# Two row streams on one core: the side work handed out by a count of VectorE's and ScalarE's time per chunk

## The chip, the core and the metric

One core of a Trainium2 chip runs the whole kernel. The metric is the device time of one execution in microseconds; lower is better. TensorE (PE) does the matrix products, VectorE (DVE) and ScalarE (ACT) the elementwise work, GpSimd (POOL) nearly nothing, and the sync engine (SP) issues the transfers.

## What is computed

The reference, cut to what matters:

```python
# attention: a causal convolution of 7 softmaxed taps per head, 8 heads of 24 columns
w = softmax(weight)                               # (8, 7)
x = einsum('hk,bskhg->bshg', w, windows_of(x))    # (2, 4096, 192)
x = x.reshape(8192, 192)
# layer 1
h = x @ moe_w_in                                  # (8192, 2048)
x = (h * clip(h + 3, 0, 6) / 6) @ moe_w_out       # (8192, 192)
# layer 2
h = x @ moe2_w_in
out = where(h > 0, h, exp(min(h, 0)) - 1) @ moe2_w_out
```

The inputs `x`, `w_in`, `w_out` of the two layers arrive as 64-bit floats, in two 32-bit words each.

## The kernel before

**Tiling.** The 8192 tokens are 16 blocks of 512 (half from each batch). The 2048 hidden columns are 16 groups of 128. A **chunk** is one group of one block of one layer: there are 2 x 16 x 16 = 512, listed in `slots` and numbered from 0. Layer 1's first blocks come first; from chunk 112 on, 16 chunks of layer 2 and 16 of layer 1 alternate; from chunk 400 on there is layer 2 alone. Every fp32 product is made of rounded (fp32r) high and low parts, so a chunk has 5 matrix products of 128 rows in `mm1` (input to hidden, with the operands opA to opD of the block) and 5 in `mm2` (hidden to output).

**Two streams.** Up to chunk 35 the matmuls use all 128 rows of the array (`whole_rows`). From chunk `BOTH + LAG` = 36 on, each product is cut into its lower and upper 64 rows, and two streams of matmuls (`lower_rows`, `upper_rows`) are issued in turn, so that a pair runs side by side. The lower stream makes the lower half of `h` in a PSUM bank, a one-element memset on POOL (`relay`, one per chunk) hands the bank on, and the upper stream adds its half. `h` has three banks (`ps_h`, `bufs=3`): the lower stream can begin chunk s + 3 only when chunk s's bank has been read.

**The main work of a chunk** on the other engines (`gate`, `split_g`): ACT makes `u` from `h`, DVE makes `g` from `u` and `h` (this frees the bank), ACT rounds the `g` of the chunk before to `gh`, and DVE makes `gl`, the remainder. In layer 2 ACT has a second pass over `u`, the exponential. `mm2` of a chunk follows five chunks later.

**The side work** also runs on DVE and ACT. It is (a) the convolution of later blocks (`conv`): per block two transposes on DVE, two products on ACT, six tap steps of 512 and six of 256 on DVE (`acc`), then ACT's copies to opA, opD, opC, DVE's remainders opB, opC, opD, and ACT's last two copies; (b) decoding and splitting the weights (`decode`, `split_w`), part by part: ACT `xw` and DVE `cw` from the raw words, DVE joins them in `xw`, ACT rounds (`wi1h`, `wi1r`, `wo`), DVE makes the remainder; (c) the sums of the two accumulators and the output transposes (`first_sum`, `second_sum`, `store`); (d) layer 2's operands (`split_y`). Both engines work in the order in which their instructions are issued.

**The planner.** Each piece of side work is a generator; a step is what it issues up to the next `yield`. After each chunk's main work `run_jobs(s)` issues steps: first those whose due chunk has come (`last(jb)`), then, as every job earns credit at its rate (cost left over chunks left), the job with the most credit, until the credits together are at most `STEP` = 300. A step's cost is DVE's metered work plus a fifth of ACT's (`step`, class `Meter`: fixed 80 or 90 plus the elements of a row). `LATER` after a step keeps the job from being stepped again in the same chunk, but from chunk 128 on only (`at[0, RA, 0]`), and not when it is due. The weights' rate comes from `due(item)`, the chunk that first needs the part. Order on the engines is as issued from chunk 36 on (`manual_schedule`); before that a scheduler places the instructions.

Of the kernel before, what the change touches and what calls it, by code (L numbers as in the profile page):

```python
# [18 lines left out]
LAG = 4  # L19
LAG2 = LAG + 1  # L20
# [7 lines left out]
ACT_LOW = range(5, 9)  # L28
R_CUTS = ((4, 4, 8), (8,))
STEP = 300  # L30
NB = 512
HB = NB // 2
SQ = 32
# [23 lines left out]
def conv_moe_moe2(ctx: ExitStack, tc: tile.TileContext, x, weight, w_in1, w_out1, w_in2, w_out2, out):  # L57
# [26 lines left out]
    assert 2 * R == P and B == 2  # L84
    JT = NB // P
    LO, UP, ALL = slice(0, R), slice(R, P), slice(0, P)
    NBLK = NT // NB

    vec, act = Meter(nc.vector, 80), Meter(nc.scalar, 90)
# [28 lines left out]
    def word(raw, i):  # L118
        return raw.rearrange("p (n two) -> p n two", two=2)[:, :, i]

    def decode(raw, n, meanwhile, low_by_vec):
# [3 lines left out]

        xw = tmp.tile([P, NB], F32, name="xw", tag="xw")
        act.activation(xw[:, :n], word(raw, 1).bitcast(F32), AF.Prelu, scale=2.0 ** -112, alpha=2.0 ** 32)
        c = tmp.tile([P, NB], I32, name="cw", tag="cw")
        low = word(raw, 0).bitcast(U32)
# [12 lines left out]
    def load_w(item):  # L142
        kind, l, a, e = item
        t = stage.tile([P, 2 * NB], I32, name="raw", tag="raw")
        if kind == "out":
# [15 lines left out]
    def split_w(item, f):  # L161

        kind, l, a, e = item
        if kind == "out":
            v = f[:, :(e - a) * D].rearrange("p (f e) -> p f e", f=e - a)
            w = wo[l][:, a:e]
            act.copy(w[:, :, 0:D], v)
            yield  # L170
            for c0, c1, to in ((0, P, 2 * P), (P, D, D)):
                vec.tensor_tensor(out=w[:, :, to:to + c1 - c0], in0=v[:, :, c0:c1],
                                  in1=w[:, :, c0:c1].bitcast(F32), op=ALU.subtract)
            yield
            return
        w = {k: v[:, a * P:e * P] for k, v in wi[l].items()}
        if kind == "in":
            f = f[:, :(e - a) * P]
            act.copy(w["h"], f)
            yield  # L180
            vec.tensor_tensor(out=w["l"], in0=f, in1=w["h"].bitcast(F32), op=ALU.subtract)
        else:
            f = f[:, :(e - a) // 2 * P].rearrange("p (f c) -> p f c", c=P)
            r = w["r"].rearrange("p (f two c) -> p two f c", two=2, c=P)
            for k, h in enumerate((LO, UP)):
                act.copy(r[h, k], f[h])
            yield
            for k, h, o in ((0, LO, UP), (1, UP, LO)):
                vec.tensor_tensor(out=r[o, k], in0=f[h], in1=r[h, k].bitcast(F32), op=ALU.subtract)
        yield  # L190


# [366 lines left out]
    def mm2(s, half, which=(0, 1, 3, 2, 4), cols=slice(0, NB)):  # L559

        l, b, f = slots[s]
        gh, gl = gs[s]
        w = wo[l][half, f, :]
        first, last = f == 0, f == NF - 1
        if first:
            acc[l, b, half is UP] = [ps_o.tile([P, NB], F32, name=f"p{i}", tag="po") for i in range(2)]
        p0, p1 = acc[l, b, half is UP]
        w0h, wr, w0l = (w[:, k * P:(k + 1) * P] for k in range(3))
        todo = [(p0, w0h, gh, 0), (p0, w0l, gh, 0), (p1, wr, gh, 0), (p0, w0h, gl, 1), (p1, wr, gl, 1)]
        for i in which:  # L570
            p, k, m, end = todo[i]
            n = R + 2 if k is wr and end and not last else P
            nc.tensor.matmul(p[:n, cols], k[:, :n], m[half, cols], start=first and not end and k is not w0l,  # L573
                             stop=end == 1 and (last and cols.stop == NB or s == NS - 2 and half is UP and p is p0))
            yield
# [11 lines left out]
    at = {sl: i for i, sl in enumerate(slots)}  # L587
# [17 lines left out]
    def step(jb, s):  # L605
        w = vec.work, act.work
        said = next(jb[2], jobs)
        done = said is jobs
        if said is LATER and s >= at[0, RA, 0]:
            jb[8] = s  # L610
        cost = vec.work - w[0] + (act.work - w[1]) // 5
        jb[4] += 1
        jb[6] += cost
        jb[7] -= cost
        if done:
            jobs.remove(jb)

    def load(item):

        kind, _, a, e = item  # L620
        n = (e - a) * {"out": D, "in": P, "r": R}[kind]
        lo = {"out": n + 160, "in": n + 80, "r": 2 * n + 160}[kind]
        return n // 2 + 80 + n + 80 + lo + (2 * n + 180) // 5

    def run_jobs(s):

        def last(jb):
            return jb[0]() - (1 if jb[0]() <= BOTH else 2)

        def rate(jb):  # L630
            if jb[3]:
                return max(jb[5] - jb[6], 0) / max(last(jb) - s, 1)
            need, most = 0, 0
            for k in range(ready[0], len(items)):
                need += load(items[k]) * (1 - min(steps[0], 3) / 4 if k == ready[0] else 1)
                most = max(most, need / max(due(items[k]) - LEAD - 1 - s, 1))
            return most

        for jb in sorted(jobs, key=lambda j: j[0]()):
            while jb in jobs and (s >= last(jb) or not jb[5] and jb[3] and s >= jb[1]):  # L640
                step(jb, s)
        for jb in jobs:
            if s >= jb[1]:
                jb[7] += rate(jb)
        while True:
            going = [j for j in jobs if s >= j[1] and s > j[8]]
            if sum(j[7] for j in going) <= STEP:
                break
            step(max(going, key=lambda j: j[7]), s)

    def whole(*gens):
        for g in gens:
            yield from g

    def drain(gen):
        for _ in gen:
            pass

    def due(item):
        kind, l, a, e = item  # L660
        return at[l, 0, a] + ((LAG, LAG2 - 2)[l] if kind == "out" else 0)

    def when(i):

        if i >= len(items):
            return 0
        return due(items[i]) - LEAD
# [42 lines left out]
    def prepare():  # L710

        last = iter(())
        for i, item in enumerate(items):
            ahead(i)
            n = (item[3] - item[2]) * {"out": D, "in": P, "r": R}[item[0]]
            f = yield from counted(decode(raws.pop(i), n, last, i not in ACT_LOW))
            ready[0], steps[0] = i, 0
            last = split_w(item, f)
            next(last)
        yield from last  # L720
        ready[0] = len(items)
# [45 lines left out]
    for b in range(2, NBLK):  # L767
        e = at[0, b, 0] - 2
        if b <= RA:
            t = at[0, b - 1, 0]  # L770
            if b > 2:
                t, e = t - 2, e + (b < RA)
            else:
                t += NF // 2
        else:
            t = at[0, b - 1, 0] - 8
            e = at[0, b - 1, NF - 1]
        job(feed(b), 1, t - 8, t - 7)
        job(whole(squares(b), conv(b)), 2 + CONV, t, e, WORK["conv"])
    for b in range(NBLK):  # L780
        e = at[1, b, 0]
# [57 lines left out]
    BOTH = at[0, 2, 0]  # L839

    def whole_rows():

        for s in range(BOTH + LAG):
            yield from mm1(s, ALL)
            first_done(s)
            if s >= LAG:
                yield from seconds_with(s - LAG, ALL)
# [28 lines left out]
    def lower_rows():  # L876

        two = seconds(LO)
        for s in range(BOTH + LAG, NS):
            yield from mm1(s, LO)  # L880
            if s >= BOTH + LAG2:
                yield from some(two, 5)
        yield from two

    def upper_rows():

        two = seconds(UP)
        yield from some(two, HEAD)
        for s in range(BOTH + LAG, NS):
            yield from mm1(s, UP)  # L890
            first_done(s)
            if s >= BOTH + LAG2:
                yield from some(two, 5)
        yield from two

    drain(whole_rows())
    with tc.manual_schedule():
        ends = {}
        n = {LO: 0, UP: HEAD}
        for half in (LO, UP):  # L900
            for s in range(BOTH + LAG, NS):
                assert half is LO or n[half] > ends[s]
                n[half] += 5 if (half is LO) == (slots[s][2] % 2 == 0) else 4
                if half is LO:
                    ends[s] = n[half]
                n[half] += 5 * (s >= BOTH + LAG2)
        going = [lower_rows(), upper_rows()]
        while going:
            for g in list(going):
                if next(g, jobs) is jobs:  # L910
                    going.remove(g)
        for k in range(B):
            drain(mm2(NS - 1, ALL, (0, 1, 3), slice(k * HB, (k + 1) * HB)))
        last_store(NBLK - 1, *(acc.pop((1, NBLK - 1, up)) for up in (False, True)))
        run_jobs(NS + 9)
# [30 lines left out]
```

## Time and profile before

| what | value |
|---|---|
| median of 3 runs | 1141.55 us (1141.54 to 1142.05) |
| the profiled execution, its own time | 1141.55 us |
| its span, first to last instruction | 1139.7 us |
| outside the span | 1.85 us |
| PE busy | 1127.6 us, 99% |
| VectorE, ScalarE busy | 81%, 82% |
| granted TensorE clock | 0.999 of full speed |

A row of the timeline gives start, duration, engine, line, operation, tiles (out<-in), shape, count and, in brackets, the engine's idle time before and what ended it. An instruction's duration includes its write-back, which overlaps the next one: queued instructions of 512 columns that last 0.69 us start 0.60 us apart. For sums along a queue the distance from start to start is used.

### The profile page before, as it was taken

How to read it: one execution, taken by the hardware profiler on the slowest of the kernel's cores; microseconds unless marked ns; L12 is line 12 of the kernel's file. 1: busy time of each engine (PE TensorE's matmuls, PEld its weight loads, DVE VectorE, ACT ScalarE, POOL GpSimd, SP SyncE). 2: the span in 40 equal slices, each digit the busy share in tenths (PEclk: the TensorE clock that was granted, in tenths of full speed). 3: DMA queues.
4: the chain of work that ended last, by engine and by line, in shares of the span. 5: the costliest groups of instructions: out<-in, count | busy, mean ns of one | idle time of the engine just before them, and what ended most of it. 6: DMA issues, size and time to landing. Idle time of an engine off the chain costs nothing.

```text
span 1139.7 us, 25118 instructions
## 1 busy us (share of the span) xinstructions
PE 1127.6 (99%) x9490; PEld 1065.4 (93%) x9490; DVE 918.5 (81%) x1558; ACT 935.1 (82%) x1699; POOL 44.5 (4%) x491
## 2 busy tenths in 40 slices
PE   8999999999999999999999999999999999999998
PEld 6787989888899999999999999999999999999997
DVE  7998999998887868779687887878867677777675
ACT  8877877778878787887878878787886899899886
POOL 0000000000000000000000000000000000000000
PEclk9999999999999999999999999999999999999999
DMA  6411121010010100101001010000000000000001
GB/s 188 108 53 42 36 49 44 29 29 1 2 29 1 21 10 2 29 1 29 2 7 23 1 29 1 16 15 1 16 1 15 2 1 16 15 15 15 9 7 28
DMA packets 105369, 26.79 MB, mean 24 GB/s; under 512 B 96416, under 2 KB 104096, under 8 KB 105248
## 3 DMA queue, kind: packets, MB, share of 16 engines
q1 hardware_dynamic: 104960, 24.99, 10.3%
q8 instruction: 74, 1.21, 0.4%
q14 instruction: 47, 0.39, 0.1%
q10 hardware_dynamic: 288, 0.20, 0.1%
HBM read 18.87 MB, written 6.29 MB: 22 GB/s over the span
## 4 chain that ended last, share of the span: by engine, by line
PE 92%; ACT 4%; DVE 3%; issue 1%; DMA 0%; ACTq 0%; SPq 0%; DVEq 0%
PE p L573 48%; PE h L527 44%; ACT u L51 1%; DVE g L51 1%; DVE gl L51 1%; DVE acc L51 0%; ACT gh L51 0%; ACT opC L51 0%; ACT xw L51 0%; ACT opD L51 0%; ACT diagl L51 0%; ACT xT L51 0%; DMA x_sq<-in_x_dram 0%; ACT acc L51 0%; DVE s L51 0%
## 5 line engine op out<-in xcount | busy, mean ns | idle before, releaser
L573 PE MATMUL p<-gh,wo 64*128 64x512 f32 (+1 forms) x2976 | 717.2, 386 | 0.0
L573 PE MATMUL p<-gl,wo 64*128 64x512 f32 (+2 forms) x1984 | 601.5, 386 | 0.0
L51 DVE SCALAR_TENSOR_TENSOR g<-u,h 128x512 f32<-128x512 f32 x512 | 350.4, 685 | 184.6 <-ACT u L51 178.2
L573 PEld LDWEIGHTS p<-gh,wo 64*128 64x128 f32 (+1 forms) x2976 | 412.9, 184 | 27.9 <-ACT gh L51 1.1
L51 DVE TENSOR_TENSOR gl<-g,gh 128x512 fp32r<-128x512 f32 x512 | 350.5, 685 | 1.9 <-ACT gh L51 1.6
L51 ACT CAST gh<-g 128x512 fp32r<-128x512 f32 x512 | 311.9, 609 | 9.6 <-DVE g L51 9.2
L51 ACT ACTIVATE u<-h,three 128x512 f32<-128x512 f32 x256 | 176.1, 688 | 107.7 <-PE h L527 105.3
L573 PEld LDWEIGHTS p<-gl,wo 64*128 64x128 f32 (+2 forms) x1984 | 252.6, 160 | 6.7 <-DVE gl L51 0.2
L51 ACT ACTIVATE u<-h 128x512 f32<-128x512 f32 x256 | 152.7, 597 | 57.5 <-PE h L527 56.2
L527 PE MATMUL h<-opA,wi1l 64*128 64x512 f32 x512 | 198.0, 387 | 0.0
L527 PE MATMUL h<-opA,wi1h 64*128 64x512 f32 x512 | 197.9, 386 | 0.0
L527 PE MATMUL h<-opB,wi1h 64*128 64x512 f32 x512 | 197.6, 386 | 0.0
L527 PE MATMUL h<-opA,wi0h 64*128 64x512 f32 (+1 forms) x476 | 183.9, 390 | 2.4 <-DVE g L51 2.1
L527 PE MATMUL h<-opA,wi0l 64*128 64x512 f32 (+1 forms) x476 | 183.3, 388 | 0.0
L527 PE MATMUL h<-opB,wi0h 64*128 64x512 f32 (+1 forms) x476 | 182.7, 387 | 0.0
L51 ACT ACTIVATE u<-u 128x512 f32<-128x512 f32 x256 | 161.9, 633 | 7.6
L527 PE MATMUL h<-opC,wi1r 64*128 64x512 f32 x384 | 148.2, 386 | 0.0
L527 PE MATMUL h<-opD,wi1r 64*128 64x512 f32 x384 | 148.2, 386 | 0.0
L527 PE MATMUL h<-opC,wi0r 64*128 64x512 f32 (+1 forms) x366 | 141.0, 387 | 0.7 <-ACT opC L51 0.6
L527 PE MATMUL h<-opD,wi0r 64*128 64x512 f32 (+1 forms) x366 | 140.8, 387 | 0.0
L51 DVE SCALAR_TENSOR_TENSOR acc<-xT,taps,acc 128x256 f32<-128x256 f32 (+1 forms) x180 | 106.8, 603 | 0.1
L527 PEld LDWEIGHTS h<-opA,wi0h 64*128 64x128 f32 (+1 forms) x476 | 87.6, 184 | 11.3 <-DVE g L51 6.5
(108 smaller groups left out, 1220.5 us busy)
## 6 DMA issues: line engine op xcount, KB each, us to landing
raw<-in_moe_w_out_dram SPq DMA_DIRECT2D x16, 384.0 KB, 3.2
out_dram<-z SPq DMA_DIRECT2D x180, 32.0 KB, 1.7
x_sq<-in_x_dram SPq DMA_DIRECT2D x112, 32.0 KB, 2.1
raw<-in_moe_w_in_dram SPq DMA_DIRECT2D x7, 512.0 KB, 3.9
raw<-in_moe_w_in_dram SPq DMA_DIRECT2D x8, 256.0 KB, 4.0
xr_sq<-in_x_dram SPq DMA_DIRECT2D x56, 32.0 KB, 2.1
x_sb<-in_x_dram SPq DMA_DIRECT2D x4, 128.0 KB, 2.9
raw<-in_moe_w_in_dram SPq DMA_DIRECT2D x4, 128.0 KB, 3.2
```

The lines of the kernel that those rows point to most:

```text
L51: return fn(*args, **kw)
L527: mm = nc.tensor.matmul(h, k, m[half], start=low and i == 0, stop=high and i == len(todo) - 1)
L573: nc.tensor.matmul(p[:n, cols], k[:, :n], m[half, cols], start=first and not end and k is not w0l, stop=end == 1 and (last and cols.stop = ...
```

## The change

1. A count `booked` of the metered work of VectorE and of ScalarE runs along; each chunk takes `SLOT` = 2153 from it. In `run_jobs` the handing-out by credit also stops when either engine's count has reached `SLOT` (`full`), from chunk 36 on. Steps that are due are issued as before.
2. `due` of layer 2's weights is twelve chunks sooner (`SOON` = 12), which raises the weights' rate in all rounds.
3. Layer 2's remainders of `wi1r` are two steps, one for each half (`yield` in `split_w`).
4. One more round of `run_jobs`, for chunk 35, at the start of the row-split stage.

```diff
--- before.py
+++ after.py
@@ -28,6 +28,8 @@
 ACT_LOW = range(5, 9)
 R_CUTS = ((4, 4, 8), (8,))
 STEP = 300
+SLOT = 2153
+SOON = 12
 NB = 512
 HB = NB // 2
 SQ = 32
@@ -187,6 +189,8 @@
             yield
             for k, h, o in ((0, LO, UP), (1, UP, LO)):
                 vec.tensor_tensor(out=r[o, k], in0=f[h], in1=r[h, k].bitcast(F32), op=ALU.subtract)
+                if l == 1 and k == 0:
+                    yield
         yield
 
 
@@ -622,6 +626,11 @@
         lo = {"out": n + 160, "in": n + 80, "r": 2 * n + 160}[kind]
         return n // 2 + 80 + n + 80 + lo + (2 * n + 180) // 5
 
+    booked = [(e, [0, 0]) for e in (vec, act)]
+
+    def full(s):
+        return s >= BOTH + LAG and any(b[0] + e.work - b[1] >= SLOT for e, b in booked)
+
     def run_jobs(s):
 
         def last(jb):
@@ -636,6 +645,8 @@
                 most = max(most, need / max(due(items[k]) - LEAD - 1 - s, 1))
             return most
 
+        for e, b in booked:
+            b[:] = max(b[0] - SLOT, 0) + e.work - b[1] if s >= BOTH + LAG else 0, e.work
         for jb in sorted(jobs, key=lambda j: j[0]()):
             while jb in jobs and (s >= last(jb) or not jb[5] and jb[3] and s >= jb[1]):
                 step(jb, s)
@@ -644,9 +655,11 @@
                 jb[7] += rate(jb)
         while True:
             going = [j for j in jobs if s >= j[1] and s > j[8]]
-            if sum(j[7] for j in going) <= STEP:
+            if sum(j[7] for j in going) <= STEP or full(s):
                 break
             step(max(going, key=lambda j: j[7]), s)
+        for e, b in booked:
+            b[:] = b[0] + e.work - b[1], e.work
 
     def whole(*gens):
         for g in gens:
@@ -658,7 +671,7 @@
 
     def due(item):
         kind, l, a, e = item
-        return at[l, 0, a] + ((LAG, LAG2 - 2)[l] if kind == "out" else 0)
+        return at[l, 0, a] + ((LAG, LAG2 - 2)[l] if kind == "out" else 0) - l * SOON
 
     def when(i):
 
@@ -895,6 +908,7 @@
 
     drain(whole_rows())
     with tc.manual_schedule():
+        run_jobs(BOTH + LAG - 1)
         ends = {}
         n = {LO: 0, UP: HEAD}
         for half in (LO, UP):
```

The matmuls keep their order. What moves is side work on ACT and DVE from about chunk 29 on, and with it the transfers that the steps issue on SP. The functions are one or two lines lower in the changed file, so helper line L51 reads L53.

**ScalarE, chunks 59 and 60: the end of block 4's convolution** (each chunk begins with `u<-h`; `acc` are the convolution's two accumulators, 512 and 256 columns). Before:

```order
L51 ACTIVATE u<-h,three 128x512
L51 CAST gh<-g 128x512
L51 CAST wo_97<-xw 128x2x192
L51 ACTIVATE xw<-raw 128x384
L51 CAST opC<-acc_1673 64x256
L51 CAST opD<-acc_1673 64x256
L51 ACTIVATE u<-h,three 128x512
L51 CAST gh<-g 128x512
L51 CAST opD<-opC 64x256
L51 CAST opC<-opD 64x256
```

Now:

```order
L53 ACTIVATE u<-h,three 128x512
L53 CAST gh<-g 128x512
L53 ACTIVATE u<-h,three 128x512
L53 CAST gh<-g 128x512
L53 CAST opC<-acc_1674 64x256
L53 CAST opD<-acc_1674 64x256
L53 CAST opD<-opC 64x256
L53 CAST opC<-opD 64x256
```

The wo and xw steps have left chunk 59, and the second pair of copies from `acc` has moved from chunk 59 to 60, in front of the last two copies.

**VectorE, chunks 57 and 58** (each begins with `g<-u,h`). Before:

```order
L51 SCALAR_TENSOR_TENSOR g<-u,h 128x512
L51 TENSOR_TENSOR gl<-g,gh 128x512
L51 SCALAR_TENSOR_TENSOR xw<-xw,cw 128x384
L51 SCALAR_TENSOR_TENSOR acc_1673<-xT_1634,taps,acc_1673 128x256
L51 SCALAR_TENSOR_TENSOR g<-u,h 128x512
L51 TENSOR_TENSOR gl<-g,gh 128x512
L51 TENSOR_TENSOR opB<-acc_1671,opA 128x512
```

Now:

```order
L53 SCALAR_TENSOR_TENSOR g<-u,h 128x512
L53 TENSOR_TENSOR gl<-g,gh 128x512
L53 SCALAR_TENSOR_TENSOR acc_1672<-xT_1603,taps,acc_1672 128x512
L53 TENSOR_TENSOR yr<-s_1756,yr 64x512
L53 SCALAR_TENSOR_TENSOR g<-u,h 128x512
L53 TENSOR_TENSOR gl<-g,gh 128x512
L53 SCALAR_TENSOR_TENSOR acc_1674<-xT_1637,taps,acc_1674 128x256
```

The last tap step of 256 has moved from chunk 57 to 58, the chunk in which ACT copies its result to opD and opC. The same stands at chunks 41, 74 and 90.

**ScalarE in layer 2's own stretch, chunks 410 to 412** (opD, opC are layer 2's operands; VectorE makes `opC<-yr,opD` in chunk 410 before, in 412 now). Before:

```order
L51 ACTIVATE u<-h 128x512
L51 ACTIVATE u<-u 128x512
L51 CAST gh<-g 128x512
L51 CAST opC<-opD 64x512
L51 ACTIVATE u<-h 128x512
L51 ACTIVATE u<-u 128x512
L51 CAST gh<-g 128x512
L51 ACTIVATE u<-h 128x512
L51 ACTIVATE u<-u 128x512
L51 CAST gh<-g 128x512
L51 CAST opD<-opC 64x512
```

Now:

```order
L53 ACTIVATE u<-h 128x512
L53 ACTIVATE u<-u 128x512
L53 CAST gh<-g 128x512
L53 CAST opD<-yr 64x512
L53 ACTIVATE u<-h 128x512
L53 ACTIVATE u<-u 128x512
L53 CAST gh<-g 128x512
L53 ACTIVATE u<-h 128x512
L53 ACTIVATE u<-u 128x512
L53 CAST gh<-g 128x512
L53 CAST opC<-opD 64x512
L53 CAST opD<-opC 64x512
```

`opD<-opC`, which reads VectorE's remainder, now stands in the same chunk as that remainder. Not shown: in chunks 61 and 93 the join of a weight part on VectorE (`xw<-xw,cw`) and ACT's rounding of that part now stand in one chunk; before there was at least one chunk between them.

## Rows read from the trace of the kernel before

**Rows 1.** Section 1 of the page: busy us, share of the span, instructions

```profile
PE 1127.6 (99%) x9490; PEld 1065.4 (93%) x9490; DVE 918.5 (81%) x1558; ACT 935.1 (82%) x1699; POOL 44.5 (4%) x491
```

**Rows 2.** Waits of the PE: us in total, times, longest us

```profile
PE h L527 <- DVE g L51: 2.1, 5, 0.8
```

**Rows 3.** Timeline of POOL: start us, us, instruction, [idle before <-releaser]

```profile
101.53 0.09 POOL L529 MEMSET relay<- 1x1 f32 x1 [0.91 <-PE h L527]
...
414.27 0.09 POOL L529 MEMSET relay<- 1x1 f32 x1 [2.18 <-PE p L573]
...
1126.91 0.09 POOL L529 MEMSET relay<- 1x1 f32 x1 [1.95 <-PE h L527]
```

**Rows 4.** Busy time by stretch: us, then each engine (x instructions), PEclk, DMA share, GB/s

```profile
162.40:197.50 35.10, 34.95 (x308) 32.16 (x306) 33.68 (x61) 27.04 (x51) 1.73 (x16) 1.00 0.17 40
```

**Rows 5.** Timeline of DVE, an odd and an even chunk without lateness

```profile
237.17 0.69 DVE L51 SCALAR_TENSOR_TENSOR g<-u,h 128x512 f32<-128x512 f32 x1 [0.24 <-ACT u L51]
...
239.21 0.69 DVE L51 SCALAR_TENSOR_TENSOR g<-u,h 128x512 f32<-128x512 f32 x1 [0.21 <-ACT u L51]
```

**Rows 6.** Timeline of PE: the matmuls that take the banks of those two chunks

```profile
239.81 0.39 PE L527 MATMUL h<-opA,wi0h 64*128 64x512 f32 x1
...
242.07 0.39 PE L527 MATMUL h<-opA,wi0h 64*128 64x512 f32 x1
```

**Rows 7.** Timeline of DVE at the start of the row-split stage

```profile
102.92 0.69 DVE L51 SCALAR_TENSOR_TENSOR g<-u,h 128x512 f32<-128x512 f32 x1 [2.78 <-ACT u L51]
```

**Rows 8.** Timeline of DVE, the end of one convolution (chunks 57 to 61)

```profile
151.35 0.54 DVE L51 SCALAR_TENSOR_TENSOR xw<-xw,cw 128x384 int32<-128x384 int32 x1
151.82 0.47 DVE L51 SCALAR_TENSOR_TENSOR acc<-xT,taps,acc 128x256 f32<-128x256 f32 x1
152.22 0.67 DVE L51 SCALAR_TENSOR_TENSOR g<-u,h 128x512 f32<-128x512 f32 x1
...
156.82 0.69 DVE L51 SCALAR_TENSOR_TENSOR g<-u,h 128x512 f32<-128x512 f32 x1 [1.26 <-ACT u L51]
...
158.03 0.41 DVE L51 TENSOR_TENSOR opC<-acc,opD 64x256 fp32r<-64x256 f32 x1
...
160.08 0.69 DVE L51 SCALAR_TENSOR_TENSOR g<-u,h 128x512 f32<-128x512 f32 x1 [0.53 <-ACT u L51]
```

**Rows 9.** Timeline of DVE, one tap step of 512 and what follows

```profile
112.76 0.75 DVE L51 SCALAR_TENSOR_TENSOR acc<-xT,taps,acc 128x512 f32<-128x512 f32 x1
113.42 0.68 DVE L51 SCALAR_TENSOR_TENSOR g<-u,h 128x512 f32<-128x512 f32 x1
```

**Rows 10.** Timeline of ACT, two heavy chunks

```profile
102.20 0.69 ACT L51 ACTIVATE u<-h,three 128x512 f32<-128x512 f32 x1 [1.81 <-PE h L527]
...
105.02 0.68 ACT L51 ACTIVATE u<-h,three 128x512 f32<-128x512 f32 x1
...
201.03 1.12 ACT L51 ACTIVATE acc<-xT,taps 128x512 f32<-128x512 f32 x2
```

**Rows 11.** Timeline of ACT, the end of that convolution (chunks 58 to 60)

```profile
152.32 0.41 ACT L51 CAST opD<-acc 64x256 fp32r<-64x256 f32 x1 [0.33 <-DVE acc L51]
...
153.17 0.69 ACT L51 ACTIVATE u<-h,three 128x512 f32<-128x512 f32 x1
...
154.26 0.51 ACT L51 CAST wo<-xw 128x384 fp32r<-128x384 f32 x1
...
155.25 0.41 ACT L51 CAST opC<-acc 64x256 fp32r<-64x256 f32 x1
...
158.47 0.41 ACT L51 CAST opD<-opC 64x256 fp32r<-64x256 f32 x1 [1.18 <-DVE opC L51]
```

**Rows 12.** Timeline of DVE, the transpose of the second input tile

```profile
199.62 0.43 DVE L51 STREAM_TRANSPOSE xT<-xr_sq 128x256 f32<-128x256 f32 x1
```

**Rows 13.** Timeline of ACT in the stretch of layer 2 alone

```profile
902.47 0.60 ACT L51 ACTIVATE u<-h 128x512 f32<-128x512 f32 x1 [0.27 <-PE h L527]
```

**Rows 14.** Timeline of DVE, the same chunk

```profile
903.77 0.69 DVE L51 SCALAR_TENSOR_TENSOR g<-u,h 128x512 f32<-128x512 f32 x1
```


## The prediction

> **What bounds the kernel now.** I read the page first: PE is busy for 1127.6 of 1139.7 us, VectorE for 81%, ScalarE for 82% [rows 1]. So the time is PE's, and only what PE waits for can be won or lost. The list of PE's waits names one wait in the row-split stage, `h` for `g`, that is, the lower stream waits for a PSUM bank until VectorE has made the `g` of three chunks before [rows 2]. Those 2.1 us are only the moments in which both streams stood. The whole loss is read from POOL's memsets, one per chunk: from chunk 180 at 414.27 to chunk 511 at 1126.91 they run 331 chunks in 712.64 us without a break, 2.153 us each; from chunk 37 at 101.53 to chunk 180 143 chunks take 312.74 us, where 143 x 2.153 is 307.9 [rows 3]. (Chunks take 2.04 and 2.27 in turn, idle time and memset together, and these 143 begin and end with a long one, so 0.1 of the difference is no loss.) So PE now loses **4.8 us**, all of it between chunks 37 and 180. In that stretch VectorE is the narrow engine: 33.68 of 35.10 us from 162.40 to 197.50, at a full granted clock [rows 4].
>
> The change adds no work worth naming: the matmuls stand in the same order, the split of wi1r into two steps adds no instruction. It decides in which chunk each side step stands. I therefore compare, stretch by stretch, what VectorE and ScalarE need from `g` to `g` with PE's 2.153.
>
> **How late `g` may be.** Two chunks without lateness show it. Chunk 97's `g` ends at 237.86 and its bank is taken at 239.81, chunk 98's at 239.90 and 242.07 [rows 5, 6]: 1.95 and 2.17 us, on average 2.06. Some 0.15 of it goes into the wake-up and the slower restart of a stopped PE (my choice; with 0 each total below is 0.15 less per stretch). So **1.9 us of lateness is free**, and everything above it stops PE. While the engines never wait for PE, PE's whole delay over a stretch is the lateness at its end less 1.9.
>
> **The price of the parts.**
>
> *The extra round and the sooner weights ahead of chunk 36* bring VectorE about 0.7 us more before the row-split stage. It stood idle for 2.78 us there, until the upper stream's first `h` [rows 7]. That hides it; without this cover it would cost at most 0.7.
>
> *A queued chunk.* VectorE's instructions start 0.60 us apart at 512 columns (`g`, `gl`), a tap step of 512 takes 0.66, one of 256 0.40 [rows 8, 9]. The planner counts 592 for each of 512 and 336 for 256, so a chunk with `g`, `gl` and two tap steps counts 2112, under SLOT, and takes 2.27 us, over PE's 2.15. The new count lets VectorE fill up without ever giving it air.
>
> *The hand-offs.* Both queues work in order, so an ACT copy that reads VectorE's work of the same chunk holds back the next `u` and with it the next `g`. From `g` to the third instruction behind it 1.21 pass (156.82 to 158.03), from `u` to `g` 0.72 [rows 7, 8, 10]. Four kinds:
> - H1, the last tap step and the copies to opD and opC in one chunk: 1.21, then 0.50 from tap to copy (151.82 to 152.32), 0.85 for two copies and 0.72 [rows 8, 11]: 3.28 from `g` to `g`. VectorE's work in it is 1.61, so 1.67 are lost. New, at chunks 41, 58, 74 and 90.
> - H2, the remainders opC, opD and ACT's last copies: 156.82 to 160.08, 3.26, with an ACT wait of 1.18 [rows 8, 11]; 1.38 lost. It is there before too (chunks 60, 76, 92); now at 44, 60, 77, 92.
> - H3, joining a weight part and rounding it in one chunk: 1.21 + 0.54 + 0.05 + 0.99 for the rounding and the next load (154.26 to 155.25) + 0.72 [rows 8, 11]: 3.51, 1.5 lost. New, at 61 and 93.
> - H4, the second transpose and ACT's product from it in one chunk, 80: 1.21 + 0.43 + 0.05 + about 0.4 (half of the pair of 1.12 that is not 512 wide) + 0.72 [rows 10, 12]: 2.8, 1.25 lost.
>
> *Chunks 36 to 44.* VectorE's instructions in the new order come to 18.8 us; H1 adds 1.67, H2 0.85 (weight remainders fill part of it), and chunk 43's two copies behind a late `u` 0.66: 22.0. PE needs 18.4 (the first two chunks of the stage stand closer). Lateness 3.7 with the 0.1 at the start, stop **1.8**.
>
> *Chunks 50 to 62.* It begins on time. VectorE 28.4, H1 1.67, H2 1.38, H3 1.5: 32.9. PE 13 x 2.153 = 28.0. Lateness 4.9, stop **3.0**.
>
> *Chunks 63 to 94.* 64 `g` and `gl` at 0.60 are 38.6, 24 tap steps 12.7, the 34 others of 0.2 to 0.7 16.2: 67.5. H1 twice, H2 twice, H3 and H4 once add 8.9, and chunk 75, where ACT has the copies of wi1r and a load as at 102.20 (2.82 from `u` to `u` [rows 10]), 0.75: 77.1. PE needs 32 x 2.153 = 68.9. The stretch begins and ends at the limit of lateness and VectorE never catches up in between, so all of it stops PE: **8.2**.
>
> *Later.* Weights are then finished, some twelve chunks sooner, so the stops around chunks 122 to 128 go (0.2 left, an H2 at 124). At chunks 140 and 141 two due operands are forced in turn, layer 2's and the convolution's: two hand-offs of 3.8 and 3.25 less 4.3, from 0.2 late: 2.95, stop 1.0. In layer 2's own stretch `g` stands 1.30 behind `u` [rows 13, 14], which leaves about 1.3 of freedom; six chunks (412, 428 and so on to 492) now have remainder and copy in one chunk, 3.75 for 2.15 to 2.27: 0.2 each, 1.2. Together **2.4**.
>
> *Transfers.* The steps take their loads along on SP, and x loads now stand between the weights'. Parts are loaded two ahead, several chunks; in that stretch the DMA engines are busy for 0.17 of the time [rows 4]. I cost them at nothing; if one came late, its reader would hold VectorE or ACT for a few us, once.
>
> **Sum.** 1.8 + 3.0 + 8.2 + 2.4 = 15.4 us of stops in place of 4.8: 10.6 more. The profiled execution's own time is 1141.55, also the median of the runs (span 1139.7 and 1.85 around it): 1152.1, put at **1152.0**.
>
> **The rivals.**
> - *The hand-offs cost nothing* (faster). If the copies found their tap steps done, chunks 36 to 44 would end 0.5 late, 50 to 62 0.4, and 63 to 94 would need 67.5 of 68.9: no stop at all, the 4.8 gone: **1136.8**. It decides at chunk 61: the hand-offs there may add 1.5 before PE stops, not 4.5. For it speaks that a full count stops steps early; against it that ACT already waits 1.18 for opC and 0.33 for a tap step one chunk back [rows 11]. 8%.
> - *Only H1 is cheaper than I think*, because lateness lets ACT catch up: without its four times 1.67 the sum is 15.4 - 6.7 = 8.7, 3.9 more than now: **1145.5**; with half of it 1148.8. 12%.
> - *No change*: what is moved falls into idle time. VectorE and ScalarE have a fifth of the span free [rows 1], and 4.8 of stops stay: **1141.5**. The Trainium skill, "Perfetto Trace Analysis", section "Identifying the Most-Contended Engine", takes occupancy as the measure for these two engines and would have nothing but PE to gain on; by that rule the result is this one. The trace speaks against it: 96% in the stretch that counts [rows 4], and idle time within a hand-off cannot be used. 5%.
> - *A late load on top*, 4 us and more: over **1156.5**. 3%.
>
> **How the numbers follow.** My case has 72%; its own range is 1148 to 1156 (hand-offs 0.25 cheaper or dearer, some fourteen of them, and the 1.9 by 0.15 in each stretch). The range of 1144.5 to 1156.5 takes in the cheap H1 and leaves out the fast and the unchanged case and the late load. A measurement of this kernel can tell about 0.2%, 2.3 us, from no change: over 1143.9 is slower. Faster 0.08, same 0.05, slower 0.87.
>
> **What would show it.** In the profile of the changed kernel POOL's memsets from chunk 37 to 180 should take about 322 us in place of 312.7, and PE should wait for `g` some 15 to 20 times: before the lower halves of chunks 45, 64, 65, 78, 86, 94, 96, 97 and 144 or 145. ACT's opD<-acc should wait for `acc` by over 1.5 us four times. Wrong it would be if those copies wait under 0.5, or if `g` is back on time at chunk 70.

## The result and the profile after

The changed kernel takes **1158.63 us** (median of 4 runs, 1157.65 to 1158.75) where the kernel before takes 1141.80 beside it: 1.0144 times the time, 95% interval 1.0129 to 1.0159. The forecast was 1152.0, with a range of 1144.5 to 1156.5: the direction was right, 6.6 us are missing. The profiled execution took 1158.75, with a span of 1157.0.

Section 1 of the page, busy us, share of the span and instructions, to be held against [rows 1]:

```profile
PE 1135.3 (98%) x9490; PEld 992.9 (86%) x9490; DVE 916.5 (79%) x1558; ACT 933.5 (81%) x1699; POOL 44.4 (4%) x491
```

The same instructions keep VectorE and ScalarE busy for as long as before (within 2 us); only the span is longer. The waits of PE (us in total, times, longest), against [rows 2]:

```profile
PE h L531 <- DVE g L53: 11.0, 20, 1.1
PE h L531 <- ACT opC L53: 1.0, 3, 0.6
PE p L577 <- DVE y L53: 0.7, 1, 0.7
```

And those of ScalarE for work of VectorE that is not the chunk's `g`, after:

```profile
ACT opD L53 <- DVE opC L53: 18.6, 20, 1.6
ACT opD L53 <- DVE acc L53: 6.4, 4, 1.8
ACT opC L53 <- DVE opD L53: 4.5, 7, 0.9
ACT opA L53 <- DVE acc L53: 3.2, 4, 1.5
```

The first two of these before (the fourth is 0.4 in one wait there, the third not listed):

```profile
ACT opD L51 <- DVE opC L51: 3.5, 3, 1.2
ACT opD L51 <- DVE acc L51: 1.0, 2, 0.7
```

Most of these are the hand-offs. The 20 waits of PE, 11.0 us, are only the moments in which both streams stood; the whole loss is read below.

Where the time went is read from POOL's memsets, as in [rows 3]; the ones at the borders of the stretches (chunks 37, 48, 67, 100, 132, 148, 404 and 511):

```profile
102.63 0.09 POOL L533 MEMSET relay<- 1x1 f32 x1 [0.91 <-PE h L531]
...
128.65 0.09 POOL L533 MEMSET relay<- 1x1 f32 x1 [3.13 <-PE h L531]
...
172.51 0.09 POOL L533 MEMSET relay<- 1x1 f32 x1 [1.96 <-PE h L531]
...
252.43 0.09 POOL L533 MEMSET relay<- 1x1 f32 x1 [2.18 <-PE p L577]
...
323.13 0.09 POOL L533 MEMSET relay<- 1x1 f32 x1 [2.18 <-PE p L577]
...
358.71 0.09 POOL L533 MEMSET relay<- 1x1 f32 x1 [2.18 <-PE p L577]
...
910.16 0.09 POOL L533 MEMSET relay<- 1x1 f32 x1 [2.18 <-PE h L531]
...
1144.27 0.09 POOL L533 MEMSET relay<- 1x1 f32 x1 [1.95 <-PE h L531]
```

The distance between two of them less 2.153 for each chunk is what PE lost, its **stops** (to 0.1, since short and long chunks alternate): from chunk 67 to 100, 252.43 - 172.51 - 33 x 2.153 = 8.9. The same for the kernel before, from its own memsets. A stop "at chunk c" lies between the memsets of chunks c and c + 1, so ahead of the lower half of c + 1.

| chunks | before | forecast | after |
|---|---|---|---|
| 37 to 48 | 1.5 | 1.8 | 2.3 |
| 48 to 67 | 1.1 | 3.0 | 3.0 |
| 67 to 100 | 1.4 | 8.2 | 8.9 |
| 100 to 132 | 0.8 | 0.2 | 1.8 |
| 132 to 148 | 0.0 | 1.0 | 1.1 |
| 148 to 404 | 0.1 | 0 | 0.3 |
| 404 to 511 | -0.1 | 1.2 | 3.7 |
| sum | 4.8 | 15.4 | 21.1 |

That is 16.3 more stops, and 1.1 us more before chunk 37 (102.63 against 101.53 in [rows 3]): together 17.4, where the two spans differ by 17.3.

The price of one hand-off came out as forecast. VectorE at chunks 58 to 61, the same place as [rows 8] (chunk 58 is H1, 60 is H2, 61 is H3):

```profile
153.48 0.67 DVE L53 SCALAR_TENSOR_TENSOR g<-u,h 128x512 f32<-128x512 f32 x1
...
154.68 0.47 DVE L53 SCALAR_TENSOR_TENSOR acc<-xT,taps,acc 128x256 f32<-128x256 f32 x1
156.75 0.69 DVE L53 SCALAR_TENSOR_TENSOR g<-u,h 128x512 f32<-128x512 f32 x1 [1.60 <-ACT u L53]
...
159.10 0.68 DVE L53 SCALAR_TENSOR_TENSOR g<-u,h 128x512 f32<-128x512 f32 x1
...
162.35 0.69 DVE L53 SCALAR_TENSOR_TENSOR g<-u,h 128x512 f32<-128x512 f32 x1 [1.19 <-ACT u L53]
...
165.84 0.69 DVE L53 SCALAR_TENSOR_TENSOR g<-u,h 128x512 f32<-128x512 f32 x1 [1.39 <-ACT u L53]
```

From `g` to `g` that is 3.27, 3.25 and 3.49 us (forecast 3.28, 3.26, 3.51). ScalarE beside it shows the first one's wait, and that `u` stands right behind the copies:

```profile
155.18 0.41 ACT L53 CAST opD<-acc 64x256 fp32r<-64x256 f32 x1 [1.57 <-DVE acc L53]
155.60 0.40 ACT L53 CAST opC<-acc 64x256 fp32r<-64x256 f32 x1
156.03 0.69 ACT L53 ACTIVATE u<-h,three 128x512 f32<-128x512 f32 x1
```

### The profile page after: what moved, and what is told of

Same layout as the page of the kernel before. It is cut to its first block, busy times and chain, and to the rows that moved or that the text cites. A ratio compares the mean times of both kernels' runs of the same rounds, so it can differ in the third digit from the quotient of the medians.

```text
span 1157.0 us, 25110 instructions
## 1 busy us (share of the span) xinstructions
PE 1135.3 (98%) x9490; PEld 992.9 (86%) x9490; DVE 916.5 (79%) x1558; ACT 933.5 (81%) x1699; POOL 44.4 (4%) x491
## 4 chain that ended last, share of the span: by engine, by line
PE 85%; DVE 6%; ACT 6%; issue 2%; DMA 0%; ACTq 0%; DVEq 0%; SPq 0%
PE p L577 43%; PE h L531 41%; ACT u L53 3%; DVE g L53 2%; DVE gl L53 2%; ACT opC L53 1%; PE psc L330 1%; DVE acc L53 1%; ACT gh L53 1%; ACT opD L53 0%; DVE opD L53 0%; DVE opC L53 0%; ACT xw L53 0%; DVE xw L53 0%; DVE wo L53 0%
## 5 line engine op out<-in xcount | busy, mean ns | idle before, releaser
L577 PE MATMUL p<-gh,wo 64*128 64x512 f32 (+1 forms) x2976 | 708.7, 387 | 0.7 <-DVE y L53 0.7
L577 PE MATMUL p<-gl,wo 64*128 64x512 f32 (+2 forms) x1984 | 591.1, 386 | 0.0
L53 DVE SCALAR_TENSOR_TENSOR g<-u,h 128x512 f32<-128x512 f32 x512 | 349.1, 682 | 204.4 <-ACT u L53 198.9
L577 PEld LDWEIGHTS p<-gh,wo 64*128 64x128 f32 (+1 forms) x2976 | 392.5, 184 | 41.7 <-ACT gh L53 1.2
L53 DVE TENSOR_TENSOR gl<-g,gh 128x512 fp32r<-128x512 f32 x512 | 349.6, 683 | 1.7 <-ACT gh L53 1.4
L53 ACT CAST gh<-g 128x512 fp32r<-128x512 f32 x512 | 312.0, 609 | 10.6 <-DVE g L53 10.3
L577 PEld LDWEIGHTS p<-gl,wo 64*128 64x128 f32 (+2 forms) x1984 | 240.8, 160 | 23.6 <-DVE gl L53 0.2
L53 ACT ACTIVATE u<-h,three 128x512 f32<-128x512 f32 x256 | 176.3, 689 | 97.4 <-PE h L531 95.9
L53 ACT ACTIVATE u<-h 128x512 f32<-128x512 f32 x256 | 152.8, 597 | 52.6 <-PE h L531 51.2
L531 PE MATMUL h<-opA,wi0h 64*128 64x512 f32 (+1 forms) x476 | 186.4, 392 | 8.8 <-DVE g L53 8.7
L531 PE MATMUL h<-opA,wi0l 64*128 64x512 f32 (+1 forms) x476 | 185.9, 391 | 0.0
L53 ACT ACTIVATE u<-u 128x512 f32<-128x512 f32 x256 | 161.8, 632 | 7.6
L53 DVE SCALAR_TENSOR_TENSOR acc<-xT,taps,acc 128x256 f32<-128x256 f32 (+1 forms) x180 | 104.1, 600 | 0.1
```

The costliest lines, as they stand in the source:

```text
L53: return fn(*args, **kw)
L531: mm = nc.tensor.matmul(h, k, m[half], start=low and i == 0, stop=high and i == len(todo) - 1)
```

## The experiments

**The question.** Theory H is the prediction's own: a chunk in which ScalarE copies what VectorE makes in that same chunk is a hand-off, and only those stop PE. The rivals: V, also in the prediction's words, that VectorE's count lets that engine fill up without air; W, that the weights due sooner give the stretch too much to do; O, that the two engines have no room, however the steps stand. A came with the trace after: that ScalarE's count holds steps back until several of one job fall into one chunk.

Each kernel was timed beside the kernel before. "Stops" is the sum from chunk 37 to 511 in its profile, in us; the hand-offs are counted from its order of issue, without seven at chunks 173 to 365 that cost nothing (below). One expectation puts those of the changed kernel at seventeen; the full list has 21.

| kernel | median us | ratio, 95% interval | stops | hand-offs |
|---|---|---|---|---|
| before | 1141.8 to 1142.6 | | 4.8 | 3 |
| changed | 1158.63 | 1.0129 to 1.0159 | 21.1 | 21 |
| no_count | 1141.15 | 0.998 to 0.9999 | 4.0 | 3 |
| count_vector_only | 1143.55 | 1.0002 to 1.002 | 6.2 | 3 |
| count_scalar_only | 1156.20 | 1.0105 to 1.0138 | 18.3 | 14 |
| no_extra_round | 1148.58 | 1.0039 to 1.0069 | 11.8 | 12 |
| pause_from_36 | 1149.22 | 1.0047 to 1.0077 | 11.8 | 13 |
| count_alone | 1159.88 | 1.014 to 1.0168 | 22.8 | 15 |
| no_sooner | 1159.17 | 1.0133 to 1.0167 | 20.5 | 15 |
| sooner_alone | 1143.10 | 0.9999 to 1.0018 | 6.2 | 5 |
| high_count | 1141.65 | 0.9985 to 1.0004 | 4.6 | 3 |
| before_pause_from_36 | 1141.05 | 0.9982 to 0.9999 | 3.7 | 0 |
| no_count_pause_from_36 | 1139.91 | 0.9972 to 0.999 | 2.8 | 0 |
| high_count_pause_from_36 | 1139.44 | 0.9965 to 0.9986 | 2.1 | 0 |

**Which part of the change costs the time.** The changed kernel without the count:

```diff
-            if sum(j[7] for j in going) <= STEP or full(s):
+            if sum(j[7] for j in going) <= STEP:
```

> The changed kernel without its count: the credits alone decide again; the sooner weights, the split step and the extra round stay. Theory H (a hand-off is a chunk in which ScalarE copies what VectorE makes in that same chunk, and only these stop PE): in its order of issue such chunks are 41, 76 and 118, three as in the kernel before (60, 76, 92), so 1141 us, 1139.5 to 1143. Theory W (the loss comes from layer 2's weights that are due twelve chunks sooner, so that VectorE has too much to do up to chunk 97): the 11 us of more stops between chunks 36 and 97 stay, 1151 or more. Theory V (VectorE's count lets that engine fill up) says the same as H here, about 1141.

1141.15 us: the count is the whole loss, and W is out. Then the count for one engine alone; of the two lines below each run has one in the place of the old:

```diff
-        return s >= BOTH + LAG and any(b[0] + e.work - b[1] >= SLOT for e, b in booked)
+        return s >= BOTH + LAG and any(b[0] + e.work - b[1] >= SLOT for e, b in booked[:1])
+        return s >= BOTH + LAG and any(b[0] + e.work - b[1] >= SLOT for e, b in booked[1:])
```

> The changed kernel with the count of VectorE alone; ScalarE's no longer stops the handing-out. Theory V (my prediction's words: the count puts 592 for tap steps that take 0.66 us, so VectorE fills up without air): the loss stays, 1152 or more. Theory H: hand-offs are left at chunks 41, 60 and 118 only, none in layer 2's own stretch, so 1142.5 us, 1141 to 1145. Theory A (ScalarE's count is what holds steps back until several of one job fall into a chunk): as H, 1142.5.

> The changed kernel with the count of ScalarE alone. Theory V: nearly nothing is lost, below 1145. Theories H and A: hand-offs at chunks 41, 44, 60, 76, 90, 92 (two kinds), 118, 124 and at six chunks of layer 2's own stretch (412 to 492), fourteen against the seventeen that matter in the changed kernel, so most of the loss stays: 1153.5 us, 1150 to 1157; layer 2's own stretch loses 3.8 us as in the changed kernel.

1143.55 and 1156.20: V falls as the account of the whole loss. Against the run without the count, VectorE's costs 2.4 us (with three hand-offs in either run) and ScalarE's 15.1 of 17.5, nearly the whole of layer 2's own stretch among it. The stops by stretch (148 to 404, with 0.1 to 0.3, is left out):

| chunks | no count | VectorE's alone | ScalarE's alone | both (changed) |
|---|---|---|---|---|
| 37 to 48 | 1.5 | 1.4 | 2.4 | 2.3 |
| 48 to 100 | 1.3 | 3.5 | 7.2 | 11.9 |
| 100 to 148 | 1.3 | 1.2 | 5.5 | 2.9 |
| 404 to 511 | -0.1 | -0.1 | 3.3 | 3.7 |

So ScalarE's count costs much by itself, but up to chunk 100 the two work together: 10.6 us more than without the count, where they cost 2.2 and 5.9 alone. The planner of the changed kernel, written out, says the same: with more than STEP of credit left, chunks 48 to 99 are ended by VectorE's count 21 times, by ScalarE's 17 times and by both twice; from chunk 404 on by ScalarE's 26 times of 32.

Layer 2's stretch shows why ScalarE's count is so strict there. The planner puts 602 for each of layer 2's three main instructions, 1806 of 2153 in each chunk, and they take 1.68 us of PE's 2.15 (924.59 to 926.27 between their starts in the profile after). The two sums at the end of a block add 1204; ScalarE then counts 3010 at chunk 403, is over the limit into chunk 405, and every further copy puts it over again. The credits that are left reach 1703 at chunk 411 and 2356 at chunk 57, where STEP would keep them at 300. From there two ways lead to a hand-off. Up to chunk 118 the pile is mostly spent as soon as there is room, on two or three steps of the one job that has most. At chunks 77, 124, 140, 141 and the six of layer 2's stretch the steps are held back until they are due, and then come together. Steps of one job follow from each other, and that is a hand-off.

The run with ScalarE's count alone has the extreme of a pile, at chunk 129: nine tap steps in one chunk, 4.98 us of VectorE. This is no hand-off, and PE stops for 1.77 us all the same, so H's "only those stop PE" is too strong. Its timelines of DVE and PE:

```profile
315.69 4.98 DVE L53 SCALAR_TENSOR_TENSOR acc<-xT,taps,acc 128x512 f32<-128x512 f32 x9
320.59 0.68 DVE L53 SCALAR_TENSOR_TENSOR g<-u,h 128x512 f32<-128x512 f32 x1
```

```profile
321.33 0.50 PE L531 MATMUL h<-opA,wi0h 64*128 64x512 f32 x1 [1.77 <-DVE g L53]
```

**The other parts.** Without the extra round, and the kernel before with the count alone or with the sooner weights alone:

```diff
-        run_jobs(BOTH + LAG - 1)
```

> The changed kernel without the extra round for chunk 35. My prediction put that round at 0, so without it the time would stay at 1158. Theory H: the round itself is cheap, but without it the steps fall otherwise and the hand-offs at chunks 41, 44, 58, 60, 61, 92 and 93 are gone; left are 74, 77, 90, 124, 140, 141 and the six of layer 2's stretch: 1148.5 us, 1146 to 1152, with nothing lost between chunks 48 and 67.

1148.58: the round costs 10 us beside the count. It adds next to nothing itself (without the count it is there too, in the run of 1141.15); it shifts every later step, and eleven hand-offs up to chunk 97 become three. Nothing is lost from 48 to 67, as expected.

```diff
+    booked = [(e, [0, 0]) for e in (vec, act)]
+    def full(s):
...
-            if sum(j[7] for j in going) <= STEP:
+            if sum(j[7] for j in going) <= STEP or full(s):
```

> The kernel before with the count alone: due times, remainders and rounds as before. Theory W (layer 2's sooner weights are at fault): 1142 to 1144. Theory A (credits that pile up while ScalarE's count is full, and are then spent on several steps of one job in one chunk, or are due): the hand-offs 42, 74, 90, 93, 94, 121, 124, 140, 141 and the six of layer 2's stretch, and piled steps at 127 and 144 as in the run with ScalarE's count alone at 132: 1156 us, 1152 to 1160.

```diff
-        return at[l, 0, a] + ((LAG, LAG2 - 2)[l] if kind == "out" else 0)
+        return at[l, 0, a] + ((LAG, LAG2 - 2)[l] if kind == "out" else 0) - l * SOON
```

> The kernel before with layer 2's weights due twelve chunks sooner, and nothing else. Theory H: hand-offs at 44, 58, 74, 92 and 118, two more than before, stops near 62, 77 and 95: 1143 us, 1141.5 to 1145. Theory W: 1150 or more.

1159.88 and 1143.10. The count needs neither the round nor the sooner weights to cost what it costs: alone it loses less up to chunk 100, but 6.3 us from 100 to 132 and 6.6 from 132 to 148, since the weights then come in when they are due. The converse, the changed kernel without the sooner weights:

> The changed kernel without the sooner due time. Theory A: the weights come in late under the count and fall due near chunks 127 and 144, as in the run with the count alone; piled steps there cost some 8 us and the hand-offs up to 100 are fewer: 1155 us, 1152 to 1158. If the sooner due time were a cost of its own under the count, the time would fall by the 5 us and more that chunks 48 to 100 lose over the kernel before: below 1150.

1159.17, 1.2 over the range that I gave and 4.2 over its middle. The mechanism is the one expected (stops of 4.7 at chunk 127, 3.5 at 144), but I had left out the clock: behind the stop at 127 PE ran at half rate for a while, which is 1.7 of the 4.2; the other 2.5 were not taken apart. Busy time by stretch of this kernel (us, then PE, PEld, DVE, ACT, POOL, PEclk, DMA share, GB/s):

```profile
305.00:307.00 2.00, 0.00 (x0) 0.00 (x0) 0.68 (x2) 1.97 (x5) 0.00 (x0) 1.00 0.00 0
307.00:309.00 2.00, 1.94 (x12) 1.60 (x14) 1.62 (x4) 1.94 (x5) 0.00 (x1) 0.73 0.00 0
309.00:311.00 2.00, 2.00 (x12) 1.54 (x12) 1.56 (x3) 1.12 (x2) 0.08 (x1) 0.50 0.00 0
311.00:313.00 2.00, 2.00 (x20) 1.68 (x18) 0.56 (x1) 1.19 (x2) 0.09 (x1) 0.92 0.00 0
```

**Is it the hand-offs, or the load?** The same count, due times and work, with one condition changed, so that steps that yield LATER are kept apart from chunk 36 on:

```diff
-        if said is LATER and s >= at[0, RA, 0]:
+        if said is LATER and s >= BOTH + LAG:
```

> The changed kernel with one line more: a job that yields LATER pauses for the rest of the chunk from chunk 36 on, not from 128 on. The work of each stretch is the same, the count too. Theory H: up to chunk 100 the hand-offs that are left are 61, 77, 93 (steps that are due) and 96, and from there 124, 140, 141 and the six of layer 2's stretch; no stop before chunk 67, some 3 between 67 and 100, so 1148.5 us, 1146 to 1151. Theory O (VectorE and ScalarE have simply too much to do in that stretch once steps are due sooner): the same work takes the same time, 1157 to 1159.

1149.22: with eight hand-offs fewer nine of the 16 us are gone, and O falls: up to chunk 100 the planner hands out the same metered work in both kernels stretch by stretch, and the stops there fall from 14.2 to 5.1. The ends of this run's memsets, chunks 37 and 511, give its 11.8:

```profile
102.10 0.09 POOL L533 MEMSET relay<- 1x1 f32 x1 [0.90 <-PE h L531]
...
1134.47 0.09 POOL L533 MEMSET relay<- 1x1 f32 x1 [1.95 <-PE h L531]
```

The Trainium skill ("Perfetto Trace Analysis", section "Identifying the Most-Contended Engine") takes occupancy as the measure for VectorE and ScalarE. Over the whole span it does not tell these kernels apart: 79% and 81% busy in the slowest, 81% and 82% in the fastest; the order of the same steps alone moves 20 us. What is left in this run are steps that are due, which LATER does not hold, and one join and rounding of a weight part at chunk 96, which does not yield it.

A higher limit, with which the count seldom ends a chunk's handing-out (12 chunks without that pause and 17 with it, where it was 156 in the changed kernel). The same constant is also what each chunk takes off the count, so both rise:

```diff
-SLOT = 2153
+SLOT = 2700
```

> The changed kernel with the count's limit at 2700 in place of 2153, without the longer pause. Theory A: ScalarE's count is then hardly ever full, no credit piles up; hand-offs left at 41, 74 and 76, none in layer 2's stretch: 1141 us, 1139.5 to 1143. Theory V (both engines filled up without air): 1158 or more.

> The changed kernel with the count's limit at 2700 in place of 2153, and LATER's pause from chunk 36 on. Theory H: no chunk hands work from VectorE to ScalarE and back any more, and nothing falls due, so no stop of over 0.1 us is left from chunk 37 on: the 4.8 us of stops of the kernel before are won, 1137.3 us, 1136.5 to 1139.5. Theory O: a limit above PE's own pace lets both engines fill up more, 1158 or more.

1141.65 and **1139.44**; the second is 0.9965 to 0.9986 of the kernel before, faster than both, with no hand-off left. Its waits of PE:

```profile
PE h L531 <- ACT opC L53: 0.8, 2, 0.6
PE h L531 <- DVE g L53: 0.8, 3, 0.3
```

The waits for opC lie ahead of chunk 37. The run did not win all 4.8 us, which I had expected: stops of 0.5 and 0.6 stay at chunks 41 and 75, both ended by `g`. At 41 it is VectorE's own load after all: from chunk 36 to 39 its queue is never empty, and the steps take more than they count (592 each):

```profile
104.11 0.75 DVE L53 SCALAR_TENSOR_TENSOR acc<-xT,taps,acc 128x512 f32<-128x512 f32 x1
104.87 0.69 DVE L53 TENSOR_TENSOR wi1r<-xw,wi1r 64x512 fp32r<-64x512 f32 x1
105.58 0.69 DVE L53 SCALAR_TENSOR_TENSOR g<-u,h 128x512 f32<-128x512 f32 x1
```

0.76 and 0.71 from start to start. So V is a real cost too, of 1 or 2 us (here, and in the run with VectorE's count alone) and not of 10. The pause without any count, and the pause alone in the kernel before:

> The changed kernel without the count, with LATER's pause from chunk 36 on: what is left of the change is the sooner weights, the split step and the extra round. Theory H: no hand-off is left, as with the limit of 2700, so the same time within 1 us: 1139.8 us, 1138.5 to 1141, and the limit of 2700 does nothing worth measuring. If a high limit is of use by itself (it stops the fullest chunks), this run is slower than that one by over 1 us.

> The kernel before with LATER's pause from chunk 36 on, and nothing else. Theory H: the three hand-offs 60, 76 and 92, each followed by a stop (0.35 to 1.2 us at chunks 63, 79, 91 and 95), are gone; the stops at 41 and around 127 stay. 1140 us, 1139 to 1141.5, nothing above 0.2 us of stops between chunks 48 and 100. Theory O: 1142, unchanged.

1139.91 and 1141.05. The limit of 2700 does nothing that these runs can tell (the intervals overlap). In the kernel before the pause takes the three hand-offs away, but a stop of 0.5 at chunk 63 and one of 1.4 at 41 remain: 3.7 us of stops without a hand-off, so half of what was expected is won; the sooner weights, the split step and the extra round together bring the other microsecond.

## Why the prediction fell short

**Right, and shown.** What bounds the kernel, and the four prices. The four H1 chunks take 3.27 or 3.29 from `g` to `g` (forecast 3.28), the four H2 3.25 (3.26), the two H3 3.49 and 3.60 (3.51), H4 2.86 (2.8), chunk 75 2.80 (2.82). Up to chunk 97 the sum was 13.0 and came out as 14.2, with stops ahead of every lower half that the forecast named (45, 64, 65, 78, 86, 94, 96, 97 and 145, of 0.6 to 1.3 us). The free lateness of 1.9 us is borne out by these sums, not measured by itself; the 0.15 in it was a choice that no run shows. PE waits for `g` 20 times (forecast 15 to 20), ScalarE's opD for `acc` four times, 1.45 to 1.81 us each (forecast over 1.5). The rival of hand-offs that cost nothing, the cheap H1 and the unchanged case are out, and no load came late: the only two waits for a transfer, 2.2 and 0.5 us in the first 10 us, are there before too (2.2 and 0.4).

**Mis-sized, and by which step.** The step that failed is the paragraph *Later*: it put 2.4 us on all that lies behind chunk 97, and the profile shows 6.9 (1.8, 1.1, 0.3 and 3.7 in the table). That is 4.5 of the 6.6 us missing; 1.2 more are missing up to chunk 97 and 1.1 ahead of chunk 37 (to 0.2 in the sum). Memsets from 37 to 180 took 325.0 us (102.63 to 427.62), not 322, and layer 2's stretch another 2.5.
- *"0.2 left, an H2 at 124"* (chunks 112 to 128) came out as 1.8. I looked there for convolution hand-offs in layer 1's way and missed chunk 118, where the last tap step of 512 and the copy to opA meet in a chunk of layer 2:

```profile
296.04 0.62 ACT L53 CAST opA<-acc 128x512 fp32r<-128x512 f32 x1 [1.51 <-DVE acc L53]
```

  It takes 3.80, and with the 3.70 of chunk 124 it stops PE at 121 for 0.3 and at 127 for 1.4. The run with ScalarE's count alone has both chunks and the same two stops; in the two with 124 but not 118 (no_extra_round and pause_from_36) the stop at 127 is 0.8 and there is none at 121. So even the H2 at 124 alone was 0.8 and not 0.2: 124 is a chunk of layer 2, where the hand-off took 3.70 and not 3.26.
- *"0.2 each, 1.2"* in layer 2's stretch was 0.34 to 0.78, together 3.7. The price was near, 3.84 to 3.86 for 3.75; the start was wrong. I let each of the six begin at no lateness, as chunk 412 nearly does. Ahead of the other five stand a sum and an output transpose of VectorE, two chunks before. Measured against PE's pace, `g` begins 0.46 later at chunk 428 and 0.16 later at 444 than at 412, and the stops behind the three are 0.78, 0.47 and 0.34: the lateness at the start is what the stop has more. Why every second one begins later still was not followed up. ScalarE and VectorE at chunk 412:

```profile
930.70 0.62 ACT L53 CAST opC<-opD 64x512 fp32r<-64x512 f32 x1
932.12 0.62 ACT L53 CAST opD<-opC 64x512 fp32r<-64x512 f32 x1 [0.80 <-DVE opC L53]
932.76 0.60 ACT L53 ACTIVATE u<-h 128x512 f32<-128x512 f32 x1
```

```profile
930.20 0.69 DVE L53 SCALAR_TENSOR_TENSOR g<-u,h 128x512 f32<-128x512 f32 x1 [0.75 <-ACT u L53]
...
931.41 0.68 DVE L53 TENSOR_TENSOR opC<-yr,opD 64x512 fp32r<-64x512 f32 x1
934.06 0.69 DVE L53 SCALAR_TENSOR_TENSOR g<-u,h 128x512 f32<-128x512 f32 x1 [1.97 <-ACT u L53]
```

- *Chunks 63 to 94* came out 0.7 dearer, 8.9 for 8.2. One wait there is of a kind that I had not listed: VectorE was so late at the end of a block that its accumulator's bank was still unread when the matmuls of the next sum wanted it.

```profile
216.28 0.50 PE L577 MATMUL p<-gh,wo 64*128 64x512 f32 x1 [0.66 <-DVE y L53]
```

  That it adds to the sum is not shown: the lower half behind it (chunk 86) began at 216.88, right behind the `g` of chunk 83, which ended at 216.83. So what the 0.7 consists of stays open.
- *Ahead of chunk 36* I put 0; the profile shows 1.1. That is not the change: the run without the count has the rest of the change, and its memset of chunk 37 comes at 101.52 (last section).

**Wrong, though the sum did not show it.** "The new count lets VectorE fill up without ever giving it air" was my reason for the hand-offs. The counts of one engine alone show that ScalarE's does most of the holding back, and VectorE's the rest, up to chunk 100 both together. And the extra round "at 0" was true of its own work, not of its effect: it decides where the count's hand-offs fall, some 10 us of them. Since I read the order of issue, which already held both effects, the sum was not hurt; as a forecast of one part of the change each would have failed.

The own range of 1148 to 1156 allowed for dearer or cheaper hand-offs and for nothing overlooked. What was overlooked behind chunk 97 was the larger error: 1.6 us from chunk 100 to 132 and 2.5 in layer 2's stretch, against 0.5 in chunks 37 to 48 and 0.7 in 67 to 100.

## What to carry to other kernels

Where in-order queues feed each other, count the places where a queue waits for what the other makes in the same round, price one from start to start, and look at how late each begins; the load of a stretch tells little by itself. A limit on handing out work lets credit pile up behind it, and the pile is spent on dependent steps of one job, unless these are kept apart. And before stopping at the stretch that one knows to be narrow, run the same count over all the others.

## What the runs showed of the hardware

- **A hand-off that fits costs nothing.** The changed kernel has H2-like chunks at 173, 205 and so on to 365, 3.25 us from `g` to `g` like the others; between chunks 148 and 404 PE lost 0.3 in all. They begin on time and nothing is queued behind them, so 1.9 us of lateness takes them up.
- **The clock after a stop.** Behind a stop of 1.08 us the granted clock stayed at 1.00 (chunk 127 of the changed kernel). Behind the stop of 1.77 us above it was 0.52 and 0.63 (322 to 324 and 324 to 326 us), and behind one of 3.99 us 0.73, 0.50 and 0.92 (rows above); 0.50 is the lower of the two levels, 1.2 GHz. The loss is the missing share, (0.48 + 0.37) x 2 and (0.27 + 0.50 + 0.08) x 2: 1.7 us each time. The length of the stop alone does not decide it. At chunk 144 count_alone and no_sooner have the same stop, and the clock fell in the first of them only (two rows each, count_alone first):

```profile
350.52 0.50 PE L529 MATMUL h<-opA,wi1h 64*128 64x512 f32 x1 [3.20 <-DVE g L53]
...
352.00:354.00 2.00, 2.00 (x12) 1.58 (x10) 1.75 (x3) 1.14 (x2) 0.00 (x0) 0.50 0.00 0
```

```profile
350.33 0.50 PE L531 MATMUL h<-opA,wi1h 64*128 64x512 f32 x1 [3.20 <-DVE g L53]
...
352.00:354.00 2.00, 2.00 (x20) 1.84 (x20) 1.56 (x3) 1.52 (x3) 0.03 (x1) 1.00 0.00 0
```

  That is the 1.6 us by which the stops of the two differ from chunk 132 to 148 (6.6 and 5.0). I had counted a stop by its length alone.
- **The first microseconds differ from one execution to the next.** Seven matmuls of 512 columns each at the start, before (first three rows) and after (last two); PE waited for 0.44 just ahead in both:

```profile
6.78 2.58 PE L326 MATMUL psc<-xT,diagh 128*128 128x512 f32 x7 [0.44 <-ACT xT L51]
9.19 1.78 PE L326 MATMUL psc<-xl,diagh 128*128 128x512 f32 x7
10.81 1.79 PE L326 MATMUL psc<-xT,diagl 128*128 128x512 f32 x7
```

```profile
6.78 3.32 PE L330 MATMUL psc<-xT,diagh 128*128 128x512 f32 x7 [0.44 <-ACT xT L53]
9.90 2.47 PE L330 MATMUL psc<-xl,diagh 128*128 128x512 f32 x7
```

  After, PE needs 5.4 us for the first fourteen (6.78 to 12.20), before 4.0 (6.78 to 10.81), though the same instructions stand ahead of it. In the fourteen profiles the second seven begin between 9.19 and 9.91 and chunk 37's memset comes between 101.52 and 102.69, whatever the kernel's part from chunk 36 on; from the start of the matmul behind the first fourteen to that memset it is 90.4 to 90.7 us in all of them, so nearly the whole spread arises here. The granted clock reads 1.00 there in both, so what sets it stays open. A single profile of this kernel carries up to 1.2 us of this; the four runs of the changed kernel are spread over 1.1.
